# Seeding a PSUM bank from ScalarE in a seven-product matrix multiply, with the relu moved from VectorE to ScalarE and the down matmuls regrouped

## The chip, the cores and the metric

The kernel runs on one core of one Trainium2 chip. The metric is the device time of one execution in microseconds (us). Engines are written as the profile has them: PE is TensorE's matmuls, PEld its weight loads, DVE is VectorE, ACT is ScalarE, POOL is GpSimd, SP is SyncE.

## The reference

Pooled attention feeds a mixture of four two-layer networks, all of which see every token:

```python
k_p = k.reshape(B, H, Sp, 8, D).mean(axis=3)          # keys and values pooled by 8
v_p = v.reshape(B, H, Sp, 8, D).mean(axis=3)
attn = softmax(q @ k_p^T / sqrt(D))                   # B=8, H=8, S=576, D=64
x = (attn @ v_p)  reshaped to (4608, 512)
p = domain_probs / (domain_probs.sum(-1) + 1e-9)
for e in range(4):                                    # w1: 512 x 1024, w2: 1024 x 512
    out += p[:, e:e+1] * (np.maximum(x @ w1[e], 0.0) @ w2[e])
```

## The kernel before

The tokens are taken in nine chunks of 512. For each chunk and expert, the first layer (`x @ w1`) is a seven-product scheme of the Strassen-Winograd kind: each quarter of the hidden tile is a sum of some of seven block products, and partial sums are shared. The work is done in 70 *quads*; in one quad all seven products are formed for two 128-row blocks, four 256-column matmuls for each product. The second layer (`down`) of the previous expert is woven between the products: 16 matmuls of 512 columns a quad, in four groups. They give PE work while ScalarE and VectorE empty the PSUM banks.

```python
    def up_seven(c, e, j, between):
        ...
        def keep(ps):                                  # ScalarE: PSUM -> SBUF, f32
            r = rpool.tile([P, 2, TH], F32, name="r")
            nc.scalar.copy(out=r[:], in_=ps[:])
            return r

        def relu_sum(out, ps, r):                      # VectorE: relu(ps + r) -> bf16
            nc.vector._custom_dve(TENSOR_ADD_SAT, out=out, in0=ps[:], in1=r[:], s0=BIG, s1=0.0)

        g, d, s = bank(), bank(), bank()
        product(c, e, j, 1, g, True)
        r1 = keep(g)
        between(0)
        product(c, e, j, 2, s, True)
        relu_sum(top[:, :, 0:TH], s, r1)
        product(c, e, j, 6, g, False)
        r2 = keep(g)
        between(1)
        product(c, e, j, 5, d, True)
        product(c, e, j, 7, g, False)
        r3 = keep(g)
        relu_sum(low[:, :, TH:NT], d, r3)
        between(2)
        product(c, e, j, 4, g, False)
        nc.scalar.activation(out=low[:, :, 0:TH], in_=g[:], func=ACT.Relu)
        between(3)
        product(c, e, j, 3, d, False)
        relu_sum(top[:, :, TH:NT], d, r2)

    def down(c, e, j, n):
        first = (0, 3, 7, 12, 16)                      # groups of 3, 4, 5, 4 matmuls
        for at in range(first[n], first[n + 1]):
            r, fc = 2 * j + at // FCH, at % FCH
            ...                                        # one 512-column matmul into sums[r]
            if fc == FCH - 1:                          # the 8th and the 16th
                merge(c, e, r, sums[r])                # e == 0: ScalarE; else VectorE
```

`between(n)` is `down(..., n)` of the step before, followed by at most a few *pieces* of the next chunk's attention (scores, exponentials, and once per chunk `opening`, which folds the keys, and `folded_values`, which folds the values; both folds are VectorE's). In the traces every engine runs its instructions in the order in which this code issues them: PE's products and down groups stand in it in all 70 quads, and so do VectorE's merges, folds and relu-sums at the folds looked at below. Two facts follow: product 2 does not touch bank `g`, so it needs nothing of `r1`; and a `merge` stands in VectorE's queue wherever the last matmul of its sum was issued.

The softmax here doesn't subtract the row's maximum and nothing guards it: scores larger than these inputs give would overflow.

## Time and profile before

| | before |
|---|---|
| time | 544.82 us, median of 3 (544.32 to 545.24) |
| profiled span | 543.2 us |
| PE, VectorE, ScalarE busy | 511.9, 322.4, 233.5 us |

The first line below is the busy line of the page; then come five of its groups (line, engine, operation, output<-input, shapes, count, then busy us and mean ns, then the engine's idle time just before them and what ended it).

```profile
PE 511.9 (94%) x3736; PEld 328.7 (61%) x3736; DVE 322.4 (59%) x599; ACT 233.5 (43%) x403; POOL 45.7 (8%) x64
...
L470 DVE CUSTOM_DVE_ANT_0 H_sb<-g_ps,r 128x512 bf16<-128x512 f32 x210 | 143.8, 687 | 162.6 <-ACT r L466 90.3
...
L466 ACT COPY r<-g_ps 128x512 f32<-128x512 f32 x210 | 123.1, 586 | 208.4 <-PE g_ps L432 206.7
L432 PE MATMUL g_ps<-xf,w_bf 128*128 128x256 bf16 x1120 | 157.6, 274 | 6.4 <-DVE H_sb L470 4.1
...
L515 DVE SCALAR_TENSOR_TENSOR acc<-o_ps,p_all,acc 128x512 f32<-128x512 f32 x108 | 80.5, 746 | 21.1 <-PE o_ps L501 21.1
...
L487 ACT ACTIVATE H_sb<-g_ps 128x512 bf16<-128x512 f32 x70 | 41.8, 598 | 48.2 <-PE g_ps L432 48.2
```

The next view gives the busy time of each engine in stretches of the span of before (from:to, length, then busy us and count for PE, PEld, DVE, ACT, POOL; PE's granted clock; DMA share; GB/s).

```profile
0.00:60.00 60.00, 40.28 (x256) 23.68 (x256) 30.85 (x70) 22.60 (x38) 26.71 (x41) 0.94 1.18 183
170.00:530.00 360.00, 357.29 (x2628) 233.32 (x2627) 210.88 (x380) 159.19 (x275) 9.78 (x12) 1.00 0.26 51
530.00:543.20 13.20, 8.27 (x41) 3.73 (x39) 4.91 (x7) 0.60 (x1) 0.00 (x0) 0.91 0.36 79
```

PE is nearly full in the long middle stretch (357.3 of 360 us). VectorE has 149 us to spare there. So a lighter VectorE gains only in the few places where PE waits for it. From the fifth quad on these are six places at the folds and two behind weight combinations before 90 us. In one of the six the chain of work that ended last passes from PE to VectorE and back (start us, length us, what; this is before, around 98 to 107 us):

```profile
97.92 0.12 PE g_ps L432
98.05 0.02 issue
98.07 0.68 DVE H_sb L470
98.75 1.14 DVE kraw L157
...
101.39 0.60 DVE H_sb L470
101.99 0.66 DVE acc L515
102.65 1.15 DVE vraw L157
...
104.88 0.74 DVE acc L515
105.62 0.61 DVE H_sb L470
106.23 0.04 issue
106.27 0.81 PE g_ps L432 x6
```

Read it from top to bottom as VectorE's queue. A relu-sum (98.07) is followed by the key fold (kraw), the next relu-sum, a merge (acc), the value fold (vraw), a second merge and the relu-sum that frees bank `d` (105.62). PE starts product 5 of the next quad at 106.27, 0.97 us late.

One caution. A 512-column matmul is shown as 380 ns long, but such matmuls start 215.7 ns apart: the record includes time in which the next one already runs. "Idle before" therefore misses a stall that is shorter than that overlap, and understates a longer one. Where stalls matter, I take them from the start times of single matmuls: the distance to the previous start, less the distance that back-to-back matmuls of that size show.

### The profile page before, as it was taken

How to read it: one execution, taken by the hardware profiler on the slowest of the kernel's cores; microseconds unless marked ns; L12 is line 12 of the kernel's file. 1: busy time of each engine (PE TensorE's matmuls, PEld its weight loads, DVE VectorE, ACT ScalarE, POOL GpSimd, SP SyncE). 2: the span in 40 equal slices, each digit the busy share in tenths (PEclk: the TensorE clock that was granted, in tenths of full speed). 3: DMA queues.
4: the chain of work that ended last, by engine and by line, in shares of the span. 5: the costliest groups of instructions: out<-in, count | busy, mean ns of one | idle time of the engine just before them, and what ended most of it. 6: DMA issues, size and time to landing. Idle time of an engine off the chain costs nothing.

```text
span 543.2 us, 9149 instructions
## 1 busy us (share of the span) xinstructions
PE 511.9 (94%) x3736; PEld 328.7 (61%) x3736; DVE 322.4 (59%) x599; ACT 233.5 (43%) x403; POOL 45.7 (8%) x64
## 2 busy tenths in 40 slices
PE   2696999999999999999999999999999999999996
PEld 1354556566656666566666665666566666666663
DVE  3725588837773767367836665568456644554453
ACT  1463343473346333643373345533653345334430
POOL 6632100200110000201100002000000000000000
PEclk9999899999999999999999999999999999999999
DMA  8999980681781014914831119331101010011003
GB/s 122 197 206 200 196 109 1 136 133 31 93 152 38 19 21 111 153 28 70 121 90 23 28 51 165 65 69 32 59 17 25 35 53 1 11 40 39 2 1 77
DMA packets 72954, 40.98 MB, mean 75 GB/s; under 512 B 42688, under 2 KB 68288, under 8 KB 72912
## 3 DMA queue, kind: packets, MB, share of 16 engines
q0 software_dynamic: 33744, 22.63, 29.2%
q1 hardware_dynamic: 39168, 17.77, 14.0%
q8 instruction: 29, 0.48, 0.4%
q14 instruction: 13, 0.11, 0.1%
HBM read 45.16 MB, written 9.44 MB: 101 GB/s over the span
## 4 chain that ended last, share of the span: by engine, by line
PE 84%; DVE 9%; DMA 5%; issue 1%; ACT 0%; POOL 0%; POOLq 0%; DVEq 0%
PE o_ps L501 41%; PE g_ps L432 36%; DMA vraw<-in_v_dram 4%; PE sc_ps L221 2%; DVE H_sb L470 2%; DVE acc L515 2%; PE h_ps L450 2%; PE c_ps L249 1%; DMA kraw<-in_k_dram 1%; DVE vraw L157 1%; DVE kraw L157 1%; DVE vraw L159 1%; PE xt_ps L261 1%; DVE kp L169 1%; DVE x_tok L236 0%
## 5 line engine op out<-in xcount | busy, mean ns | idle before, releaser
L501 PE MATMUL o_ps<-w_bf,H_sb 128*128 128x512 bf16 x1152 | 295.6, 380 | 0.0
L470 DVE CUSTOM_DVE_ANT_0 H_sb<-g_ps,r 128x512 bf16<-128x512 f32 x210 | 143.8, 687 | 162.6 <-ACT r L466 90.3
L432 PEld LDWEIGHTS <-w_bf 128*128 128x128 bf16 x1960 | 185.3, 98 | 75.7 <-issue 11.7
L466 ACT COPY r<-g_ps 128x512 f32<-128x512 f32 x210 | 123.1, 586 | 208.4 <-PE g_ps L432 206.7
L432 PE MATMUL g_ps<-xf,w_bf 128*128 128x256 bf16 x1120 | 157.6, 274 | 6.4 <-DVE H_sb L470 4.1
L501 PEld LDWEIGHTS <-H_sb 128*128 128x128 bf16 x1152 | 113.0, 98 | 76.6 <-issue 0.8
L432 PE MATMUL g_ps<-xT,w_bf 128*128 128x256 bf16 x744 | 101.8, 273 | 0.0
L515 DVE SCALAR_TENSOR_TENSOR acc<-o_ps,p_all,acc 128x512 f32<-128x512 f32 x108 | 80.5, 746 | 21.1 <-PE o_ps L501 21.1
L487 ACT ACTIVATE H_sb<-g_ps 128x512 bf16<-128x512 f32 x70 | 41.8, 598 | 48.2 <-PE g_ps L432 48.2
L228 ACT ACTIVATE expT<-sc_ps 72x512 bf16<-72x512 f32 x64 | 37.1, 592 | 12.5 <-PE sc_ps L221 12.3
L236 DVE TENSOR_TENSOR x_tok<-c_ps,inv 128x256 bf16<-128x256 f32 x72 | 30.6, 425 | 2.5
L92 POOL DMA_DIRECT2D q_sb<-in_q_dram x9 | 7.9, 876 | 237.1 <-DMA qT<-q_sb 230.2
L512 ACT ACTIVATE acc<-o_ps,p_all 128x512 f32<-128x512 f32 x36 | 24.9, 691 | 4.7 <-PE o_ps L501 4.7
L249 PEld LDWEIGHTS <-expT 72*128 72x128 bf16 x256 | 16.2, 102 | 15.3 <-issue 3.1
L235 DVE RECIPROCAL inv<-c_ps 128x4 f32<-128x4 f32 x72 | 12.7, 177 | 14.6 <-PE c_ps L249 11.9
L249 PE MATMUL c_ps<-vp,expT 72*128 72x65 bf16 x256 | 18.4, 200 | 2.8 <-DVE vp L188 2.5
L221 PE MATMUL sc_ps<-qT,kpT 64*72 64x256 bf16 x128 | 14.5, 298 | 1.4 <-DVE qT L210 0.9
L182 PE MATMUL kpt_ps<-ident,kp 72*128 72x72 bf16 x16 | 1.5, 251 | 14.4 <-DVE kp L169 14.4
L221 PEld LDWEIGHTS <-kpT 64*72 64x72 bf16 x128 | 5.4, 111 | 13.8 <-issue 12.9
L157 DVE TENSOR_TENSOR kraw<-kraw 72x2048 bf16<-72x2048 bf16 (+1 forms) x9 | 9.9, 1096 | 5.8 <-DMA kraw<-in_k_dram 5.8
L432 PE MATMUL g_ps<-x_rem,w_bf 128*128 128x256 bf16 x96 | 13.3, 273 | 0.0
L157 DVE TENSOR_TENSOR vraw<-vraw 72x2048 bf16<-72x2048 bf16 (+1 forms) x9 | 9.9, 1095 | 3.7 <-DMA vraw<-in_v_dram 3.7
(54 smaller groups left out, 140.9 us busy)
## 6 DMA issues: line engine op xcount, KB each, us to landing
out_dram<-acc SPq DMA_DIRECT2D x32, 256.0 KB, 2.5
w_bf<-in_moe_w_dram POOLq DMA_DIRECT2D x16, 256.0 KB, 11.3
w_bf<-in_moe_w_dram POOLq DMA_DIRECT2D x4, 1024.0 KB, 18.3
kraw<-in_k_dram POOLq DMA_DIRECT2D x7, 576.0 KB, 10.3
vraw<-in_v_dram POOLq DMA_DIRECT2D x7, 576.0 KB, 11.8
q_sb<-in_q_dram POOLq DMA_DIRECT2D x7, 512.0 KB, 6.9
out_dram<-acc SPq DMA_DIRECT2D x8, 128.0 KB, 2.3
kraw<-in_k_dram POOLq DMA_DIRECT2D x2, 288.0 KB, 5.8
```

Source lines behind the costliest of these rows:

```text
L157: nc.vector.tensor_add(out=raw[:, hs, 0:4, :], in0=raw[:, hs, 0:4, :], in1=raw[:, hs, 4:8, :])
L221: nc.tensor.matmul(both[r2][0:SP, hh], lhsT=kpT[lo:lo + D, h, 0:SP], rhs=qT[lo:lo + D, h])
L228: nc.scalar.activation(out=state[("expT", b)][:, 2 * pair:2 * pair + 2, :, r2, :], in_=state[("sc", b, pair)][r2][0:SP], func=ACT.Exp, sca ...
L236: nc.vector.tensor_tensor(out=x_tok[:, half], in0=c_ps[:, :, 0:D], in1=inv[:].unsqueeze(2).to_broadcast([P, NPAIR, D]), op=ALU.mult,)
L249: nc.tensor.matmul(c_ps[:, i, :], lhsT=expT[:, h, r // 2, r % 2, :], rhs=vp[:, h, :])
L432: nc.tensor.matmul(bank[:, t, :], lhsT=w1_bf[:, e, block, kc, lo:lo + P], rhs=x[:, kc, :], start=(first and t == 0 and kc == 0), stop=(t = ...
L466: nc.scalar.copy(out=r[:], in_=ps[:])
L470: nc.vector._custom_dve(TENSOR_ADD_SAT, out=out, in0=ps[:], in1=r[:], s0=BIG, s1=0.0)
L487: nc.scalar.activation(out=low[:, :, 0:TH], in_=g[:], func=ACT.Relu)
L501: nc.tensor.matmul(sums[r][:], lhsT=hidden[(c, e)][:, fc, r * P:(r + 1) * P], rhs=w2_bf[:, e, fc, :], start=(fc == 0), stop=(fc == FCH - 1),)
L512: nc.scalar.activation(out=accs[(c, r)][:], in_=o_ps[:], func=ACT.Copy, scale=prob)
L515: nc.vector.scalar_tensor_tensor(out=dst, in0=o_ps[:], scalar=prob, in1=dst, op0=ALU.mult, op1=ALU.add,)
```

## The change

The intent: form the sum of products 1 and 2 in PSUM itself. ScalarE copies product 1 into bank `s`, product 2 accumulates there, and ScalarE applies the relu. VectorE loses a third of its relu-sums. The price is a new dependency: product 2 must now wait for the copy. One down matmul is therefore moved ahead of it, from the third group to the first.

```diff
         product(c, e, j, 1, g, True)
-        r1 = keep(g)
+        nc.scalar.copy(out=s[:], in_=g[:])
         between(0)
-        product(c, e, j, 2, s, True)
-        relu_sum(top[:, :, 0:TH], s, r1)
+        product(c, e, j, 2, s, False)
+        nc.scalar.activation(out=top[:, :, 0:TH], in_=s[:], func=ACT.Relu)
...
-        first = (0, 3, 7, 12, 16)
+        first = (0, 4, 8, 12, 16)
```

## The prediction

> **What bounds the kernel now.** TensorE: the page gives PE 94% busy (511.9 of 543.2 us); in the busy times by stretch it has 357.3 of 360 us between 170 and 530 us, VectorE 210.9, ScalarE 159.2. Most missing PE time lies in the first 60 us and the last 13. Elsewhere PE stalls rarely: six times for 0.7 to 1.0 us (about 5 us) where VectorE folds keys and values, and about 1 us at weight combinations before 90 us. VectorE's relief can win at most some 8 us, 1.5%.
>
> **What changes.** VectorE loses 70 relu-sums (687 ns each, 48 us). ScalarE gains 70 relus (598 ns each, like the existing one, 42 us); 70 copies now write PSUM. I cost these at the measured 586 ns; the Trainium skill, "ScalarE: Activation LUTs" (what happens when an exp ACTIVATE runs), says ScalarE reaches PSUM faster than SBUF, so perhaps less; before's trace has no such write. Each would then be near 51% busy.
>
> **New waits.** Product 2 may start only when the copy is done. From single instructions: the copy starts 309 ns after the start of product 1's last matmul and ends at 896; PE starts about 50 ns after a releasing ScalarE instruction ends: 946. Before, product 2 starts at 756 behind three 512-column matmuls; a fourth (216 ns) makes it 972. Margin 26 ns: just hidden. The fourth comes from the gap between products 7 and 4, which falls from 1188 to 972 against the same 946. Where an exp delays the copy (three quads) about 0.2 us each is lost. Where a quad's first merge is a ScalarE copy, it now precedes the third keep: 0.1 to 0.2 us in some ten quads.
>
> **A merge moves.** Each quad's first merge is now issued after the second group of down matmuls, so on VectorE's queue it stands before the key fold instead of after it. At the six fold sites the fold waits for it and starts 1.1 to 1.5 us later in its quad. The next relu-sum ends near 6.9 to 7.4 us after product 1, where product 3 wants it at 5.75 to 6.3: a new stall of about 1.2 us before product 3, with 0.1 left of the old one before product 5. About 1.27 us a site against 0.7 to 1.0: 2.5 us more in all. Saved: 0.2 us at two or three weight combinations, perhaps 0.7 us of backlog at 57 to 75 us.
>
> **Sum.** +2.5 (folds) +0.6 (exps) +1 (merges) -1.3 = about +2.5 us.
>
> **Predicted time: 547 us, 543.5 to 552.** Faster by over 2%: 0.01; within 2%: 0.95; slower by over 2%: 0.04.
>
> **What would show it.** Relu-sums 210 to 140, relus of g_ps 70 to 140; VectorE busy down about 47 us, ScalarE up about 42, PE within 1%. PE's g_ps matmuls waiting for VectorE's relu-sum about 7 us over six places, now before product 3; product 2 near 972 ns without idle in most quads.
>
> **What would make it wrong.** The 26 ns margins are met 140 times. A copy into PSUM 100 ns longer, or delayed by its extra waits, costs 70 x 75 ns = 5 us, and twice that if the third keep is late too. If the folds find other idle VectorE time, the result is equal or about 3 us faster. Accumulating onto engine-written data relies on has_written bits set by earlier matmuls (the skill, "PSUM — Partial Sum Buffer", Terms); no trace shows it.

A note on the first page that the prediction cites: the remark on PSUM stands one heading further down on that page of the Trainium skill, "ScalarE: Activation LUTs", under Step-by-step: what each stage is for. The trace of after agrees with it, and the gain is small: the copy of 128x512 f32 into PSUM takes 570 ns in 63 of 70 quads (the group's mean is 572), the copies of the same size into SBUF take 576 to 587.

## The result

| | before | after |
|---|---|---|
| time, median | 545.03 us of 4 (544.32 to 545.53) | 549.76 us of 4 (548.79 to 550.21) |
| profiled span | 543.2 us | 548.0 us |
| ratio | 1 | 1.0085 (95%: 1.0067 to 1.0103) |

A ratio is the mean time of one kernel's runs over that of the other's of the same rounds, so it is not quite the ratio of the medians quoted beside it. The result is correct, and slower by 0.85%: inside the 2% band and inside the predicted range (543.5 to 552).

Busy line and groups of after:

```profile
PE 512.5 (94%) x3736; PEld 327.2 (60%) x3736; DVE 279.6 (51%) x529; ACT 268.0 (49%) x473; POOL 45.6 (8%) x64
...
L470 DVE CUSTOM_DVE_ANT_0 H_sb<-g_ps,r 128x512 bf16<-128x512 f32 x140 | 96.1, 686 | 118.0 <-ACT r L466 93.1
L515 DVE SCALAR_TENSOR_TENSOR acc<-o_ps,p_all,acc 128x512 f32<-128x512 f32 x108 | 81.0, 750 | 119.6 <-PE o_ps L501 119.6
...
L432 PE MATMUL g_ps<-xT,w_bf 128*128 128x256 bf16 x744 | 101.7, 272 | 6.5 <-DVE H_sb L470 6.3
L474 ACT COPY g_ps<-g_ps 128x512 f32<-128x512 f32 x70 | 40.1, 572 | 67.7 <-PE g_ps L432 67.1
L477 ACT ACTIVATE H_sb<-g_ps 128x512 bf16<-128x512 f32 x70 | 41.8, 597 | 47.4 <-PE g_ps L432 47.3
```

The work went where it was meant to go: VectorE's relu-sums fell by 47.7 us, ScalarE gained 40.3 us in copies and relus. The busy times of the engines changed by less than the forecast of 47 and 42 us, -42.8 and +34.5: the page counts time in which the records of two instructions overlap once. But look at what PE waits for. Before, 4.1 us of waiting for VectorE stood with the products that read `xf` (product 5). Now 6.3 us stand with those that read `xT` (product 3). And VectorE's merges (L515) now wait 119.6 us for PE where they waited 21.1 before: the merge has become an early instruction in VectorE's queue, at which that queue stands still. The middle stretch of after, in the columns used above:

```profile
170.00:530.00 360.00, 355.74 (x2613) 230.86 (x2612) 177.85 (x326) 184.70 (x327) 9.74 (x12) 1.00 0.26 51
```

PE lost 1.55 us more in this stretch than before although VectorE is 33 us lighter. The chain of after at the same fold as above:

```profile
99.86 0.88 PE o_ps L501 x4
100.74 0.02 issue
100.77 0.75 DVE acc L515
101.52 1.14 DVE kraw L157
102.65 0.02 issue
102.68 0.70 DVE kraw L159
103.38 0.02 issue
103.40 0.76 DVE kp L169 x2
104.16 0.61 DVE H_sb L470
104.77 0.04 issue
104.81 1.03 PE g_ps L432 x8
```

The merge comes first and waits for the last matmul of its sum. Only then do the key fold and the relu-sum behind it follow, and product 3, which needs bank `d` from that relu-sum, starts at 104.81, 1.21 us late. The same 1.21 us stands at all six folds.

Splitting the span by single instructions gives one more reading. From the first matmul of the fifth quad to the start of the last matmul the kernel before takes 466.9 us (71.0 to 537.9) and after takes 469.8 (73.0 to 542.8). I call this the *steady part*. The other 2.0 us of this pair of profiles arose before the fifth quad, and half of it before the first quad, where the code that runs is the same in both kernels.

### The profile page after: what moved, and what is told of

It reads as the page before. It is cut to its first block, busy times and chain, and to the rows that moved or that the text cites. A ratio compares the mean times of both kernels' runs of the same rounds, so it can differ in the third digit from the quotient of the medians.

```text
span 548.0 us, 9079 instructions
## 1 busy us (share of the span) xinstructions
PE 512.5 (94%) x3736; PEld 327.2 (60%) x3736; DVE 279.6 (51%) x529; ACT 268.0 (49%) x473; POOL 45.6 (8%) x64
## 4 chain that ended last, share of the span: by engine, by line
PE 84%; DVE 8%; DMA 6%; POOL 1%; issue 1%; ACT 0%; POOLq 0%; DVEq 0%
PE o_ps L501 41%; PE g_ps L432 37%; DMA vraw<-in_v_dram 6%; PE sc_ps L221 2%; PE h_ps L450 2%; DVE acc L515 1%; PE c_ps L249 1%; DVE kraw L157 1%; DVE H_sb L470 1%; DVE kp L169 1%; DVE kraw L159 1%; PE xt_ps L261 1%; DVE x_tok L236 0%; DVE vraw L157 0%; POOL q_sb L92 0%
## 5 line engine op out<-in xcount | busy, mean ns | idle before, releaser
L470 DVE CUSTOM_DVE_ANT_0 H_sb<-g_ps,r 128x512 bf16<-128x512 f32 x140 | 96.1, 686 | 118.0 <-ACT r L466 93.1
L515 DVE SCALAR_TENSOR_TENSOR acc<-o_ps,p_all,acc 128x512 f32<-128x512 f32 x108 | 81.0, 750 | 119.6 <-PE o_ps L501 119.6
L466 ACT COPY r<-g_ps 128x512 f32<-128x512 f32 x140 | 81.5, 582 | 66.1 <-PE g_ps L432 66.1
L474 ACT COPY g_ps<-g_ps 128x512 f32<-128x512 f32 x70 | 40.1, 572 | 67.7 <-PE g_ps L432 67.1
L477 ACT ACTIVATE H_sb<-g_ps 128x512 bf16<-128x512 f32 x70 | 41.8, 597 | 47.4 <-PE g_ps L432 47.3
L487 ACT ACTIVATE H_sb<-g_ps 128x512 bf16<-128x512 f32 x70 | 41.8, 597 | 41.7 <-PE g_ps L432 41.7
## 6 DMA issues: line engine op xcount, KB each, us to landing
vraw<-in_v_dram POOLq DMA_DIRECT2D x7, 576.0 KB, 12.4
```

The costliest lines, as they stand in the source:

```text
L474: nc.scalar.copy(out=s[:], in_=g[:])
L477: nc.scalar.activation(out=top[:, :, 0:TH], in_=s[:], func=ACT.Relu)
L515: nc.vector.scalar_tensor_tensor(out=dst, in0=o_ps[:], scalar=prob, in1=dst, op0=ALU.mult, op1=ALU.add,)
```

## The experiments

Eight kernels; each was timed in five rounds against the kernel before on the same chip, and all gave correct results. The first four share one set of runs of the kernel before (median 545.01), the second four another (545.52). A difference below is called one where the interval of its ratio leaves out 1. (One run of the first set of the kernel before took 550.18 us; it is in the mean.) The line numbers in these kernels' profiles move by a few lines.

The table collects the medians and the stalls before product 2, 6, 5 and 3, summed over the quads from the fifth on, from single instructions as said above. Products 1, 7 and 4 show under 1 us in every kernel. About 0.85 us in each of the columns for products 2 and 3, and 0.5 in that for product 5, is there in every kernel. It stands behind attention pieces, where the shape of the matmuls changes; that it is no wait is not shown, but it does not differ between the kernels.

The profiles of e1 to e4 lack 66 of the 3736 matmul records, 65 of them down matmuls. In e2, e3 and e4 the last down matmul before product 3 is one of these in three quads (7, 23 and 39, counted from 0): four weight loads stand there, three matmuls, and a gap of just one matmul (0.216 us). These 0.65 us are no stall and are left out of the table.

| kernel | before p2 | before p6 | before p5 | before p3 | steady part us | median us | ratio (95%) |
|---|---|---|---|---|---|---|---|
| before | 0.9 | 2.1 | 5.5 | 1.0 | 466.9 | 545.0 / 545.5 | 1 |
| after | 2.0 | 1.4 | 0.5 | 8.6 | 469.8 | 549.8 | 1.0085 (1.0067 to 1.0103) |
| e1_split_only | 0.9 | 1.5 | 1.1 | 8.6 | 469.6 | 549.1 | 1.0066 (1.0033 to 1.0100) |
| e2_merge_late | 2.0 | 1.8 | 0.5 | 0.9 | 462.5 | 540.4 | 0.9898 (0.9867 to 0.9930) |
| e3_seed_4354 | 2.0 | 1.6 | 0.5 | 0.9 | 462.6 | 541.1 | 0.9913 (0.9878 to 0.9947) |
| e4_seed_old_split | 12.4 | 1.8 | 0.5 | 0.9 | 472.8 | 550.2 | 1.0080 (1.0046 to 1.0115) |
| e5_after_again | 1.9 | 1.4 | 0.5 | 8.6 | 469.7 | 549.3 | 1.0069 (1.0039 to 1.0099) |
| e6_5344_late | 0.8 | 1.4 | 0.5 | 0.9 | 461.3 | 539.6 | 0.9892 (0.9867 to 0.9917) |
| e7_split_4354 | 0.9 | 1.7 | 6.2 | 1.7 | 468.0 | 546.3 | 1.0013 (0.9988 to 1.0038) |
| e8_relu_vector | 1.5 | 1.8 | 4.8 | 1.7 | 467.3 | 545.1 | 0.9996 (0.9969 to 1.0023) |

Theory A: the loss comes from the first merge, which the new split of the down matmuls put ahead of the key fold on VectorE's queue. Theory B, its rival: the loss comes from the seed, that is from the copy that product 2 waits for and from the added load on ScalarE.

### The new split alone (e1_split_only)

```diff
-        first = (0, 3, 7, 12, 16)
+        first = (0, 4, 8, 12, 16)      # in the kernel before; nothing else
```

> The kernel before with only the redistribution of the down matmuls (4, 4, 4, 4 in place of 3, 4, 5, 4); relu-sums stay on VectorE, nothing is copied into PSUM. Theory A (the first merge, moved ahead of the key fold on VectorE's queue, causes the new stalls): product 3 waits for VectorE's relu-sum for about 1.2 us at each of the six fold sites, the old stall before product 5 shrinks to 0.1 us, and the time is about 2 us over the kernel before (ratio near 1.004). Theory B (the seed copy and the added relu on ScalarE cause it): no new stall before product 3, ratio 1.000 or a little less, since the fourth matmul only adds slack before product 2.

Measured: 549.1 us, ratio 1.0066. The line of its waits (engine, line, for whom: us in total, times, longest):

```profile
PE g_ps L432 <- DVE H_sb L470: 6.3, 6, 1.1
```

It is the number of after, without any seed, and the steady part agrees (469.6 against 469.8). Six stalls of 1.21 us stand before product 3; those before product 5 have shrunk to 0.10 us each, as expected. Theory A holds, and the redistribution alone costs what the whole change costs. The time came out 2 us above the expectation; the steady part is 2.7 us over before, and the rest lies outside it (see e5).

### The merge issued later, all else as changed (e2_merge_late)

```diff
     def down(c, e, j, n):
         first = (0, 4, 8, 12, 16)
+        if n == 2 and held:
+            merge(*held.pop())
...
             if fc == FCH - 1:
-                merge(c, e, r, sums[r])
+                if n == 1:
+                    held.append((c, e, r, sums[r]))
+                else:
+                    merge(c, e, r, sums[r])
```

> The changed kernel with one thing undone: the first merge of each quad, though its sum is complete after the second group of down matmuls, is issued at the start of the third group, so that it stands after the key fold on VectorE's queue and after the third keep on ScalarE's, as before. Matmul order is that of the changed kernel. Theory A: the six stalls of 1.2 us before product 3 go, at most about 0.1 us is left before product 5, and the time is about 6 to 7 us below the changed kernel, near 543 us, that is 2 us below the kernel before (ratio 0.996). Theory B: it stays near 549 (ratio 1.008).

Measured: 540.4 us, ratio 0.9898: 9.4 us below the median of after, and 1% below the kernel before. The matmuls are in the same order as in after; only one instruction's place in the queues differs in each quad. Its chain at the same fold never leaves PE (the line with x3 is one of the places where a matmul record is missing; the 0.05 us behind it is part of that gap):

```profile
99.16 0.87 PE g_ps L432 x8
100.03 0.86 PE o_ps L504 x4
100.90 0.44 PE g_ps L432 x4
101.33 0.65 PE o_ps L504 x3
101.98 0.05 issue
102.03 1.04 PE g_ps L432 x8
```

and VectorE's instructions there, from the instructions in order of time (start us, length us, engine, line, operation), show why:

```profile
98.33 1.21 DVE L157 TENSOR_TENSOR kraw<-kraw 72x2048 bf16<-72x2048 bf16 x1
99.58 0.69 DVE L159 TENSOR_TENSOR kraw<-kraw 72x1024 bf16<-72x1024 bf16 x1
...
100.30 0.76 DVE L169 TENSOR_TENSOR kp<-kraw 72x512 bf16<-72x512 bf16 x2
...
100.98 0.68 DVE L470 CUSTOM_DVE_ANT_0 H_sb<-g_ps,r 128x512 bf16<-128x512 f32 x1
...
101.58 0.74 DVE L521 SCALAR_TENSOR_TENSOR acc<-o_ps,p_all,acc 128x512 f32<-128x512 f32 x1
```

The fold now starts at 98.33, while PE is still on the second down group; the relu-sum that product 3 needs ends at 101.66, before product 3 starts at 102.03, and the merge (L521 here) follows it. The steady part fell by 7.3 us: the stalls before product 3 fell by 7.7 (8.6 to 0.9), those before product 6 rose by 0.4. I had expected 543; the steady part shows that the fold term was sized about right. The other 2 us of the 9.4 lie outside the steady part (see e5).

### Another split with the merge late (e3_seed_4354)

```diff
-        first = (0, 4, 8, 12, 16)
+        first = (0, 4, 7, 12, 16)      # in the changed kernel
```

> The changed kernel with the down matmuls split 4, 3, 5, 4: the seed copy keeps its fourth matmul, taken now from the gap between products 6 and 5, and the first merge falls into the third group again. Theory A: as with the late merge, near 543 us (ratio 0.996), no stall before product 3, and product 7 does not wait (its keep ends about 1050 ns after product 6, which it may use from about 1190). Theory B: near 549.

Measured: 541.1 us, ratio 0.9913, steady part 462.6. Taking the fourth matmul from the second group instead of the third keeps the eighth matmul, and so the merge, in the third group. It needs no held merge and gives the same steady part as e2: the place of the merge decides, not how it is brought about.

### The seed without the fourth matmul (e4_seed_old_split)

```diff
-        first = (0, 4, 8, 12, 16)
+        first = (0, 3, 7, 12, 16)      # in the changed kernel
```

> The changed kernel with the old split 3, 4, 5, 4, so without the fourth matmul that hides the seed copy. The copy ends about 935 ns after the start of product 1's last matmul (measured in the changed kernel) and PE starts 50 ns later, at 985, where product 2 could start at 756: a stall of about 0.23 us in nearly all 70 quads, 14 to 16 us; the fold stalls go, since the merge is back in the third group. Time about 557 us, ratio 1.02 to 1.025. If the copy were not on the critical path, it would be near 543.

Measured: 550.2 us, ratio 1.0080. The mechanism is as expected: the median stall before product 2 is 228 ns. The chain of this kernel in one quad without attention shows the seed on the critical path:

```profile
265.19 0.89 PE g_ps L432 x8
266.07 0.02 issue
266.10 0.02 ACTq L474
266.11 0.04 issue
266.15 0.58 ACT g_ps L474
266.73 0.04 issue
266.77 1.03 PE g_ps L432 x8
```

The size was off. The stalls before product 2 came to 12.4 us, not to 0.9 + 14 or more, since in some quads attention matmuls stand between products 1 and 2 and cover the wait; and the forecast of 557 started from after's first time, which held about 2 us more outside the steady part than this kernel does. The view of waits of this kernel counts only 0.8 us of PE waiting for the seed copy: stalls of 228 ns are mostly hidden by the overlap in the records, as cautioned above. So the fourth matmul was needed, and its price as placed was the merge.

### The changed kernel once more (e5_after_again)

No edit.

> The changed kernel, unedited, once more: its second profile tells how far the first 65 us vary by themselves. If the 2 us that the first profile showed before the fifth quad are chance in the start-up loads, the fold of the first reloaded values starts anywhere between 56 and 59 us and the rest, from the fifth quad to the last matmul, again takes about 469.8 us against 466.9 before. If the change itself delays the start, the fold starts near 58.7 again. Time 548 to 550 either way.

Measured: 549.3 us, ratio 1.0069. The steady part is 469.7 us, as in the first profile (469.8). The fold of the first reloaded values, which waits for its load, began at 56.6 us here and at 58.7 us there; in the other profiles it lies between 56.3 and 57.6, in before at 56.8. So the start-up, in which the loads move about 200 GB/s, varies by some 2 us in the profiles of one and the same kernel. But chance in the start-up may not be all: the two medians are 4.7 and 3.8 us over before, the steady part 2.9. Mean time less the steady part of the one profile is 79.5 to 79.9 us in the three kernels with 4, 4, 4, 4 and the early merge (after, e1, e5; 16 runs), 78.7 in before (26 runs) and 77.4 to 78.6 in the six others, with standard errors of 0.2 to 0.6. So about 1 us more of the loss seems to go with the early merge, outside the steady part; where it arises no profile shows.

### Five matmuls ahead of product 2, merge late (e6_5344_late)

```diff
-        first = (0, 4, 8, 12, 16)
+        first = (0, 5, 8, 12, 16)      # in e2_merge_late
```

> The late merge of the run before, with five down matmuls between product 1 and product 2 and three between products 6 and 5 (5, 3, 4, 4). Product 2 is then free at about 1190 ns against the 985 at which the copy is usable, so the 13 ns in most quads and the 0.2 us in three quads behind an exp go: p2's stalls fall by about 1.1 us, product 7 (free about 1190 against 1050) does not wait. Time about 1 us below the late merge, near 539.3, ratio 0.988. If that wait was not what it seemed, no difference from the late merge.

Measured: 539.6 us, ratio 0.9892. The stalls before product 2 fell from 2.0 to the floor of 0.8 us and the steady part by 1.2 us, as expected. The medians of e2 and e6 come from different rounds and their ratios overlap, so the timing alone would not tell them apart. The middle stretch of its profile:

```profile
170.00:530.00 360.00, 360.00 (x2642) 234.65 (x2641) 180.10 (x332) 183.15 (x325) 9.77 (x12) 1.00 0.26 51
```

PE's records leave no idle time in these 360 us (they overlap, so a stall shorter than the overlap would not show). Like e2 and e3 this version beats both kernels, and its steady part is the shortest. Its time is lower by 1.1% and 1.8%: 1 - 0.9892, and 1 - 0.9892/1.0069 against the changed kernel.

### The late split without the seed (e7_split_4354)

```diff
-        first = (0, 3, 7, 12, 16)
+        first = (0, 4, 7, 12, 16)      # in the kernel before
```

> The kernel before (relu-sum on VectorE, no seed) with the split 4, 3, 5, 4: the fourth cell of a square, seed or no seed, merge in the second or in the third group. Theory A: the first relu-sum still stands before the key fold, the merge after it, so the six stalls before product 5 stay at 0.7 to 1.0 us and the time is that of the kernel before, ratio 1.000 within 0.3%. If the split alone had made the late-merge kernels fast, it would be near 0.991.

Measured: 546.3 us, ratio 1.0013. Within the expectation; the split alone makes nothing fast. One detail was missed: the stalls before product 5 are 0.92 us in three of the places where they were 0.71, as product 2, and with it the relu-sum ahead of the key fold, comes one matmul (0.22 us) later. With e1 and e3 this completes a square, in steady parts: without seed 468.0 (late) and 469.6 (early), with seed 462.6 (late) and 469.8 (early; after). The seed is worth 5.4 us with the merge late and nothing with it early.

### The seed with the relu on VectorE (e8_relu_vector)

```diff
-        nc.scalar.activation(out=top[:, :, 0:TH], in_=s[:], func=ACT.Relu)
+        nc.vector.tensor_scalar_max(out=top[:, :, 0:TH], in0=s[:], scalar1=0.0)   # in e2_merge_late
```

> The late merge with the relu of the seeded sum on VectorE again (one operation from PSUM, about 0.6 to 0.7 us) and the seed copy kept on ScalarE. If the late merge is fast because VectorE has nothing to do ahead of the key fold, the fold waits for this relu again, the stalls before product 5 come back at 0.5 to 0.9 us in six places, and the time is near the kernel before, 545 (ratio 1.000). If it is fast for another reason (the seed, the merge's place alone), it stays near 540.5 (ratio 0.990).

Measured: 545.1 us, ratio 0.9996. With one VectorE operation back ahead of the key fold, the stalls before product 5 return at 0.67 to 0.76 us in six places, and the gain in time goes with them. So the late merge is fast because VectorE has nothing to wait for ahead of the fold; keeping the sum in PSUM is by itself worth nothing here (ratio 0.9969 to 1.0023).

## Why the prediction was right or wrong

- **Right: the range and the main mechanism.** It said +2.5 us, mostly from a merge that moves ahead of the key fold. The steady part grew by 2.9 us. The new stall before product 3 was put at about 1.2 us and measured 1.21 six times, 7.3 us by start times (6.3 in the view of waits), where "about 7 us over six places" was written. The old stalls (5.05 us) went entirely, where 0.1 us a place was left over; the fold term is then +2.2 in place of +2.5. e1 produces this loss without the seed and e2 removes it with the seed.
- **Right: the exps.** Three quads behind an exp lose 203 to 205 ns each before product 2: 0.6 us, as predicted. e6 removes them.
- **Too optimistic: "Margin 26 ns: just hidden."** The copy was costed with the start of the old copy, 309 ns after the start of product 1's last matmul. It starts at 365, 56 ns later, and takes 570 instead of 586 ns, so it ends at 935 and product 2 starts at 985 to 987 in 39 quads, against 972: a stall of 13 ns, about 0.5 us in all. Its "extra waits" had been named as a risk. Before, the late-coming wait for PE sat on the copy itself; now the copy waits for ScalarE's own earlier relu, and the wait for PE sits on a separate instruction ahead of it. That this is what costs the 56 ns is read from the records, not tested by an edit.
- **Wrong in size: "0.1 to 0.2 us in some ten quads" for ScalarE merges.** The third keep is delayed by 190 ns in six quads, but there attention matmuls between products 7 and 4 cover all but some 20 ns of it, and the stalls before product 4 rose by less than 0.1 us. The term of +1 us is not there.
- **Wrong in part: the saving of 1.3 us.** The stalls behind weight combinations fell by 0.7 us (2.1 to 1.4 before product 6), less 0.27 us for a new one before product 3 in the sixth quad. The "0.7 us of backlog" cannot be seen, as the start-up there varies by more.
- **In part luck: how near the sum came.** In the steady part the terms measured +2.2 (folds), +0.6 (exps), +0.5 (the margin), under +0.1 (merges) and -0.4 (the saving), where +2.5, +0.6, 0, +1 and -1.3 were written. A cost that did not come, a saving that came in part and a cost that was not counted nearly cancel: +2.9 measured against +2.5.
- **Not foreseen: how much of the timed difference is no part of the steady run.** The medians differ by 4.7 and 3.8 us, the steady parts by 2.9. The profiles show a start-up that varies by 2 us; by the means about 1 us of the rest seems to be systematic, and its place is not known (see e5).
- **Missed: where the gain was.** The prediction capped the worth of a lighter VectorE at about 8 us and saw the moved merge as a cost to be added. It did not ask for the order that gives the cap back: with the merge late (e2, e3, e6) more than half of it is real, 4.4 to 5.6 us in the steady part.

## What to carry to other kernels

When matmuls are regrouped to hide one latency, follow every instruction that hangs on the regrouped ones into the other engines' queues: an in-order queue stops at an instruction that is issued early and ready late, and whatever was busy filling that gap (here a 2.7 us key fold) starts late. An engine that is half idle can still hold up the critical one through its order, so ask for each stall which instruction stands ahead of the releasing one, and try moving that before changing the arithmetic. And when a latency is hidden by a margin of tens of nanoseconds, count the waits on the new instruction as well as its length.

## What the Trainium skill lacked or had wrong

- "PSUM — Partial Sum Buffer", Summary: rules for kernel authors, says of a bank seeded by VectorE or ScalarE that the seed must be 0 on trn2. Here the seed is product 1, which is not zero, and all seeded kernels (after, e2 to e6, e8) gave correct results. By the code, no matmul with a start flag touches the bank between seeds, and earlier matmuls had written all of it, which agrees with the same page's account of has_written; the rule in the Summary is stricter.
- "Perfetto Trace Analysis", Identifying Dependency Chains, says that an instruction with several waits may get a semaphore instruction ahead of it, without its cost. Where the wait that comes last sat on that instruction, the copy began 56 ns later (365 against 309 ns; 44 ns later, at 353, in e8), which used up a margin of 26 ns.
- "ScalarE: Activation LUTs", Rules for kernel authors, sends relu to VectorE, which it has faster in bf16. Here, from f32 in PSUM to bf16, the relu takes 597 ns on ScalarE and 687 on VectorE (e8), and which engine's queue it stands in counts for more: with the relu on VectorE 545.1 us (ratio 0.9996), on ScalarE 540.4 us (0.9898).
